# Two transformer layers with sliding-window attention on one core: all work put in order by a list scheduler, scores in 64-key blocks on row groups of the array

## The chip, the cores and the metric

The kernel runs on one core of a Trainium2 chip. The metric is device microseconds of one launch, the median of several runs. The core has five engines with queues of their own: PE (TensorE, matrix products into PSUM), ACT (ScalarE), DVE (VectorE), POOL (GpSimd) and SP (which here only issues DMAs). Each engine runs its instructions in the order in which they were written, and waits on semaphores for the others.

## The reference

Two passes over x of 2048 rows by 512 features, each of an attention block and a feed-forward block with the same weights:

```python
def _A_ref(x, wqkv, wo):          # x normed; H = 32, Dh = 16, W = 256
    q, k, v = ...                 # x @ wqkv, split in 32 heads of 16
    scores = einsum("bhqd,bhkd->bhqk", q, k) * Dh ** -0.5
    mask = (idx[:, None] - idx[None, :] >= 0) & (idx[:, None] - idx[None, :] < W)
    p = softmax(where(mask, scores, -1e9))
    o = einsum("bhqk,bhkd->bhqd", p, v)
    return o.reshape(B, S, D) @ wo
def _B_ref(x, w1, w2):            # Dff = 1792
    return relu(x @ w1) @ w2
x = A_x
for _ in range(2):
    x = x + _A_ref(layernorm(x), A_wqkv, A_wo)
    x = x + _B_ref(layernorm(x), B_w1, B_w2)
```

## The kernel before

x lies in SBUF as `x_sb`, 16 blocks of 128 rows by 512, fp32. The work is done in eight steps k, a chunk of 512 rows of one layer each (`NCH` = 4 chunks, two layers). A step has three parts.

- `qkv_chunk` (from L167) norms the chunk (`layer_norm_chunk`, L138), turns it with DMA transposes (L164; the first chunk on the array, L159) into `xnT`, and makes `QT`, `KT` and `Vaug` by 48 matmuls of 128x512 (L176, L184, L191), which DVE takes out of PSUM (L178, L186, L193).
- `attention_qblock` (from L205) works on 128 queries. A tile of `KT` holds 8 heads of 16 features on its 128 partitions. So that one matmul gives one head, `isolate_q` (L197) copies each head's rows of Q into `Qi`, which is zero elsewhere, by 16 DMAs a step. For each t (8 heads) and each of up to three blocks of 128 keys, two matmuls (L223) give 128 keys x (8 heads x 128 queries) in PSUM, two such buffers, and one ACT exponential of 128x1024 (L225) brings them to `pt`. POOL cuts the diagonal block and the oldest one with affine_select (L228, L232). Then 24 small matmuls a t (L240, 17 columns, with `pt` as weights) add up the product with V and the sum of the exponentials. DVE divides (L247, L248), three DVE operations and two of POOL guard the result (L252 to L259).
- `attn_post` (L328) turns O by a DMA transpose (L330), multiplies it with wo (L333) and adds (L334). `ffn_chunk` (L338) norms, 56 matmuls (L346) with a ReLU on DVE (L348), 56 matmuls (L353), an addition (L355), and in the second layer the output DMA (L357).

The order is Tile's, by priority classes: scores first, then the rest of attention, then the next chunk's QKV, then the FFN of the chunk before. At the start 28 matmuls keep PE busy, ACT and DVE cast x from bf16 to fp32 (L84, L369), ACT zeroes `Qi` (L372). The last lines hold an exact way of attention, taken only if a sum of exponentials leaves its bounds (`final_flag`, L279); it is not taken here.

Of the kernel before, what the change touches and what calls it, by code (L numbers as in the profile page):

```python
# [9 lines left out]
FP32 = mybir.dt.float32  # L10
# [5 lines left out]
P = 128  # L16
NOSYNC = mybir.DependencyInfo(mybir.DependencyClass.NoSync, mybir.DependencyReason.DATA)


@with_exitstack  # L20
def kernel(
# [32 lines left out]
    CLS = {"setup": 0, "s": 1, "a": 2, "q": 3, "f": 4}
    counters = {k: 0 for k in CLS}
    cur_cls = [None]

    class prio:
        def __init__(self, cls):
            self.cls = cls  # L60
        def __enter__(self):
            self.prev = cur_cls[0]
            if self.prev is not None:
                counters[self.prev] = tc.cur_priority - CLS[self.prev] * 10_000_000
            cur_cls[0] = self.cls
            tc.cur_priority = CLS[self.cls] * 10_000_000 + counters[self.cls]
        def __exit__(self, *a):
            counters[self.cls] = tc.cur_priority - CLS[self.cls] * 10_000_000
            cur_cls[0] = self.prev
            if self.prev is not None:  # L70
                tc.cur_priority = CLS[self.prev] * 10_000_000 + counters[self.prev]

    with prio("setup"):
        nc.scalar.preload_act_table_set("natural_log_exp_and_others")
        x_sb = const.tile([P, NB, D], FP32, name="x_sb")
        x_in = A_x.rearrange("b (n p) d -> p (b n) d", p=P)
        wqkv = const.tile([P, KC, 3 * D], BF16, name="wqkv")
        wqkv_in = A_wqkv.rearrange("(kc p) n -> p kc n", p=P)
        xst0 = work.tile([P, 4, D], BF16, name="xst0", tag="xnT", bufs=1)
        nc.sync.dma_start(xst0[:], x_in[:, 0:4, :])  # L80
        for part in range(3):
            nc.sync.dma_start(wqkv[:, :, part * D:(part + 1) * D], wqkv_in[:, :, part * D:(part + 1) * D])
        for j in range(4):
            nc.scalar.copy(x_sb[:, j, :], xst0[:, j, :])  # L84
        Qi = [const.tile([P, 4, 8, 256], BF16, name=f"Qi{i}") for i in range(2)]
        wo = const.tile([P, KC, D], BF16, name="wo")
        nc.scalar.dma_start(wo[:], A_wo.rearrange("(kc p) n -> p kc n", p=P))
        w1 = const.tile([P, KC, DFF], BF16, name="w1")
        nc.scalar.dma_start(w1[:], B_w1.rearrange("(kc p) n -> p kc n", p=P))
        w2 = const.tile([P, NF, D], BF16, name="w2")  # L90
        nc.scalar.dma_start(w2[:], B_w2.rearrange("(f p) n -> p f n", p=P))
        nc.gpsimd.tensor_scalar(out=wqkv[:, :, 0:D], in0=wqkv[:, :, 0:D], scalar1=0.25, scalar2=1.0,
                                op0=ALU.mult, op1=ALU.mult)

        LN_PRESCALE = 2.0 ** -40
# [12 lines left out]

    ident = const.tile([P, P], BF16, name="ident")
    with prio("setup"):  # L110
        make_identity(nc, ident[:])
    with prio("f"):
        warm = ps_w.tile([P, 512], FP32, name="warm", tag="ps_w")
        for _ in range(N_WARMUP):
            nc.tensor.matmul(warm[:], lhsT=ident[:], rhs=ident[:].rearrange("p (o q) -> p o q", o=1).to_broadcast([P, 4, P]),
                             start=True, stop=True)
    ones_bf = const.tile([P, P], BF16, name="ones_bf")
    hm = const.tile([P, 8], FP32, name="hm")
    maskbias = const.tile([P, 3, P], FP32, name="maskbias")

    def fallback_constants():
        nc.vector.memset(ones_bf[:], 1.0)
# [5 lines left out]
        nc.vector.memset(maskbias[:], 0.0)  # L128
# [5 lines left out]

    last_startup_act = [None]

    def layer_norm_chunk(c, xnT, sfx, startup=False, j0=0, j1=4):
        mv4 = small.tile([P, 4, 2], FP32, name="mv4" + sfx)  # L138
        for j in range(j0, j1):
            b = 4 * c + j  # L140
            st = small.tile([P, 6], FP32, name="st" + sfx)
            nc.vector.bn_stats(out=st[:], in_=x_sb[:, b, :])
            nc.vector.bn_aggr(out=mv4[:, j, :], in_=st[:])  # L143
        lnv = small.tile([P, 4], FP32, name="lnv" + sfx)
        rstd = small.tile([P, 4], FP32, name="rstd" + sfx)
        with prio("setup"):
            nc.scalar.activation(lnv[:, j0:j1], mv4[:, j0:j1, 1], ACT.Ln, bias=ln_bias[:], scale=LN_PRESCALE)  # L147
            nc.scalar.activation(rstd[:, j0:j1], lnv[:, j0:j1], ACT.Exp, bias=exp_bias[:], scale=-0.5)
        nb = small.tile([P, 4], FP32, name="nb" + sfx)
        nc.vector.scalar_tensor_tensor(out=nb[:, j0:j1], in0=mv4[:, j0:j1, 0], scalar=-1.0, in1=rstd[:, j0:j1],  # L150
                                       op0=ALU.mult, op1=ALU.mult)
        for j in range(j0, j1):
            b = 4 * c + j
            xn = work.tile([P, D], BF16, name="xn" + sfx, bufs=2)
            if startup:
                nc.scalar.activation(xn[:], x_sb[:, b, :], ACT.Identity, bias=nb[:, j:j + 1], scale=rstd[:, j:j + 1])
                tp = ps_d.tile([P, KC, P], BF16, name="tp", tag="ps_d")
                for kc in range(KC):
                    nc.tensor.transpose(tp[:, kc, :], xn[:, kc * P:(kc + 1) * P], ident[:])  # L159
                last_startup_act[0] = nc.scalar.copy(xnT[:, :, j * P:(j + 1) * P], tp[:])  # L160
            else:
                nc.gpsimd.tensor_scalar(out=xn[:], in0=x_sb[:, b, :], scalar1=rstd[:, j:j + 1],  # L162
                                        scalar2=nb[:, j:j + 1], op0=ALU.mult, op1=ALU.add)
                nc.sync.dma_start_transpose(out=xnT[:, :, j * P:(j + 1) * P],  # L164
                                            in_=xn[:].rearrange("p (kc d) -> p kc d", kc=KC))
# [275 lines left out]
```

## Time and profile before

| | us |
|---|---|
| three runs | 641.25, 642.2 (median), 643.69 |
| span of the profiled execution | 643.3 |
| PE, ACT, POOL, DVE busy | 576.2, 368.2, 367.7, 321.1 |
| mean granted clock of PE, of full speed | 0.970 |
| first exponential, last exponential's group, last matmul (start) | 28.7, about 568, 634.4 |

No other time is listed for the profiled execution; its span lies among the three runs. In the rows, PE is the matmul and PEld its weight load. A matmul's duration runs from issue to its modelled end, and matmuls overlap, so the pitch of a row of them is read from a row's whole length. "idle before <- X" is the time for which the engine stood still, and what ended it.

### The profile page before, as it was taken

The numbers are of one execution on the slowest core, as the hardware profiler recorded it, in microseconds if no ns is written. First come the engines' busy times: TensorE is split into PE (matmuls) and PEld (weight loads), VectorE is DVE, ScalarE is ACT, GpSimd is POOL, SyncE is SP. The second block draws the span as 40 slices with busy tenths as digits, with TensorE's granted clock in tenths as the row PEclk, the third lists the DMA queues.
The fourth block names the chain that finished last, engine by engine and source line by source line (L and its number), as shares of the span: only waits on it lengthen the run. The fifth ranks groups of instructions, "written<-read, shape, count | busy, mean of one in ns | idle before, by whom it ended". The sixth has DMA issues, their size and how long they took to land.

```text
span 643.3 us, 12352 instructions
## 1 busy us (share of the span) xinstructions
PE 576.2 (90%) x5053; PEld 282.8 (44%) x5053; DVE 321.1 (50%) x701; ACT 368.2 (57%) x407; POOL 367.7 (57%) x391
## 2 busy tenths in 40 slices
PE   6957979999989999999899999999998899979994
PEld 2323434544544444534453444534454344534442
DVE  2794533544465634476455634475443544436361
ACT  5667686999850399705870399705894079920000
POOL 2168778888861287815872287814887147851200
PEclk8968996999999999999999999999999999999998
DMA  9601121111002110102101110202102210131302
GB/s 316 202 22 34 31 55 42 26 34 43 10 9 42 45 31 10 43 8 50 34 11 41 42 34 11 42 10 52 23 10 57 36 25 9 19 59 16 58 8 39
DMA packets 69217, 27.10 MB, mean 42 GB/s; under 512 B 52512, under 2 KB 68640, under 8 KB 69152
## 3 DMA queue, kind: packets, MB, share of 16 engines
q1 hardware_dynamic: 63984, 19.94, 13.6%
q0 software_dynamic: 2304, 2.10, 2.2%
q10 hardware_dynamic: 2864, 4.19, 1.8%
q8 instruction: 41, 0.67, 0.5%
q14 instruction: 24, 0.20, 0.1%
HBM read 7.86 MB, written 2.10 MB: 15 GB/s over the span
## 4 chain that ended last, share of the span: by engine, by line
PE 32%; POOL 19%; DMA 11%; issue 10%; ACT 8%; DVE 4%; SPq 0%; POOLq 0%; ACTq 0%
DMA OT<-O 9%; ACT pt L225 8%; PE ps_d L353 7%; POOL pt L228 7%; PE Sps L223 5%; PE ps_d L346 5%; POOL O L259 4%; POOL pt L232 4%; PE ps_w L333 3%; PE ps_d L176 3%; PE acc L240 3%; PE ps_d L184 3%; PE ps_d L191 3%; POOL O L257 2%; DMA xn2T<-xnB 1%
## 5 line engine op out<-in xcount | busy, mean ns | idle before, releaser
L225 ACT ACTIVATE pt<-Sps 128x1024 bf16<-128x1024 f32 x360 | 344.8, 1025 | 95.3 <-PE Sps L223 82.8
L223 PE MATMUL Sps<-Qi,KT 128*128 128x512 bf16 x720 | 218.9, 386 | 4.1 <-ACT pt L225 2.8
L228 POOL TENSOR_SCALAR_AFFINE_SELECT pt<-pt 128x1024 bf16<-128x1024 bf16 x128 | 140.3, 1099 | 67.4 <-ACT pt L225 67.1
L232 POOL TENSOR_SCALAR_AFFINE_SELECT pt<-pt 128x1024 bf16<-128x1024 bf16 x112 | 122.2, 1091 | 34.4 <-ACT pt L225 31.4
L240 PEld LDWEIGHTS <-pt 128*128 128x128 bf16 x2880 | 100.2, 96 | 87.6 <-POOL pt L228 38.4
L240 PE MATMUL acc<-Vaug,pt 128*128 128x17 bf16 x2880 | 108.9, 171 | 26.4 <-POOL pt L228 20.7
L346 PE MATMUL ps_d<-xn2T,w 128*128 128x512 bf16 x448 | 123.9, 378 | 0.9 <-DVE hT L348 0.9
L348 DVE TENSOR_SCALAR hT<-ps_d 128x512 bf16<-128x512 f32 x112 | 77.1, 689 | 61.4 <-PE ps_d L346 61.0
L353 PE MATMUL ps_d<-w,hT 128*128 128x512 bf16 x448 | 105.7, 381 | 0.0
L223 PEld LDWEIGHTS <-KT 128*128 128x128 bf16 x720 | 64.3, 97 | 68.5 <-issue 16.8
L334 DVE TENSOR_TENSOR x_sb<-ps_w,x_sb 128x512 f32<-128x512 f32 x32 | 22.1, 692 | 102.2 <-PE ps_w L333 80.8
L353 PEld LDWEIGHTS <-hT 128*128 128x128 bf16 x448 | 43.2, 98 | 50.4 <-issue 1.9
L346 PEld LDWEIGHTS <-w 128*128 128x128 bf16 x448 | 39.8, 97 | 43.2 <-issue 5.7
L333 PE MATMUL ps_w<-wo,OT 128*128 128x512 bf16 x128 | 38.3, 390 | 18.4 <-DMA OT<-O 18.3
L162 POOL TENSOR_SCALAR xnB<-x_sb,rstdB,nbB 128x512 bf16<-128x512 f32 x32 | 24.4, 766 | 42.4 <-DMA xn2T<-xnB 25.5
L247 DVE RECIPROCAL chk<-acc 128x16 f32<-128x16 f32 x64 | 16.4, 256 | 56.8 <-PE acc L240 56.7
L162 POOL TENSOR_SCALAR xnA<-x_sb,rstdA,nbA 128x512 bf16<-128x512 f32 x28 | 21.4, 769 | 40.2 <-DVE nbA L150 37.7
L178 DVE CAST QT<-ps_d 128x512 bf16<-128x512 f32 x32 | 22.0, 689 | 37.2 <-PE ps_d L176 37.2
L147 ACT ACTIVATE lnvB<-mv4B,ln_bias 128x4 f32<-128x4 f32 x8 | 2.4, 296 | 66.2 <-DVE mv4B L143 66.2
L357 POOL DMA_DIRECT2D out_dram<-x_sb x16 | 9.1, 570 | 52.8 <-DVE x_sb L355 37.2
L176 PE MATMUL ps_d<-xnT,wqkv 128*128 128x512 bf16 x128 | 36.4, 399 | 2.6 <-DVE QT L178 1.8
L355 DVE TENSOR_TENSOR x_sb<-ps_d,x_sb 128x512 f32<-128x512 f32 x32 | 22.0, 689 | 28.4 <-PE ps_d L353 25.8
(62 smaller groups left out, 391.5 us busy)
## 6 DMA issues: line engine op xcount, KB each, us to landing
Qi<-QT SPq DMA_DIRECT2D x128, 32.0 KB, 2.0
w<-in_B_w_dram ACTq DMA_DIRECT2D x2, 1792.0 KB, 13.9
xst<-in_A_x_dram SPq DMA_DIRECT2D x4, 512.0 KB, 14.4
out_dram<-x_sb POOLq DMA_DIRECT2D x16, 128.0 KB, 2.3
wqkv<-in_A_wqkv_dram SPq DMA_DIRECT2D x3, 512.0 KB, 13.1
wo<-in_A_wo_dram ACTq DMA_DIRECT2D x1, 512.0 KB, 5.5
OT<-O SPq DMA_TRANSPOSE x32, 2.3
xn2T<-xnB SPq DMA_TRANSPOSE x32, 2.4
```

Of the source, the lines that this page charges most:

```text
L162: nc.gpsimd.tensor_scalar(out=xn[:], in0=x_sb[:, b, :], scalar1=rstd[:, j:j + 1], scalar2=nb[:, j:j + 1], op0=ALU.mult, op1=ALU.add)
L176: nc.tensor.matmul(ps[:], lhsT=wqkv[:, kc, t * P:(t + 1) * P], rhs=xnT[:, kc, :], start=(kc == 0), stop=(kc == KC - 1))
L223: nc.tensor.matmul(Sps[:, xh].rearrange("p j q -> p (j q)"), lhsT=KT[:, t, kcols], rhs=Qih[:, t, 4 * xh:4 * xh + 4, qcols], start=True, st ...
L225: nc.scalar.activation(pt[:, kbi].rearrange("p j q -> p (j q)"), Sps[:].rearrange("p x j q -> p (x j q)"), ACT.Exp)
L228: nc.gpsimd.affine_select(out=pt[:, 2], in_=pt[:, 2], pattern=[[0, 8], [1, P]], compare_op=ALU.is_ge, fill=0.0, base=0, channel_multiplier=-1)
L232: nc.gpsimd.affine_select(out=pt[:, 0], in_=pt[:, 0], pattern=[[0, 8], [-1, P]], compare_op=ALU.is_gt, fill=0.0, base=0, channel_multiplier=1)
L240: mm = nc.tensor.matmul(acc[:, h % 16, :], lhsT=pt[:, kbi, j, :], rhs=Vaug[:, slot(layer, kb), h, :], start=(ii == 0), stop=(ii == len(kbi ...
L259: nc.gpsimd.tensor_tensor(out=O3, in0=O3, in1=ok[:].to_broadcast([P, 32, 16]), op=ALU.mult)
L333: nc.tensor.matmul(ps[:], lhsT=OT[:, kc, :], rhs=wo[:, kc, :], start=(kc == 0), stop=(kc == KC - 1))
L346: nc.tensor.matmul(ps[:, n0:n1], lhsT=w1[:, kc, f * P:(f + 1) * P], rhs=xnT[:, kc, n0:n1], start=(kc == 0), stop=(kc == KC - 1))
L348: nc.vector.tensor_relu(hT[:, f, n0:n1], ps[:, n0:n1])
L353: nc.tensor.matmul(ps[:], lhsT=hT[:, f, j * P:(j + 1) * P], rhs=w2[:, f, :], start=(f == 0), stop=(f == NF - 1))
```

## The change

The whole body is written anew; what is computed stays.

- Scores. K is kept as `KBD`: for 64 keys and one group of 32 partitions (two heads), the 64 columns of the even head and the 64 of the odd one, each zero on the other head's rows (`spread_k` does this out of PSUM with a mask of the partition's parity; two operations). A score matmul has 32 rows, 128 columns (2 heads x 64 keys) and streams up to 512 queries; four of them, one a group of 32 partitions, write four PSUM banks. Q is used as it is. A unit is one t and 512 queries (256 in the first and the last step, `HALVED`); its 12 blocks of 64 keys are packed in five groups (`FULL`; three in `HALF`) of at most 512 columns, in which only the queries lie that see the keys. There is one score buffer of four banks, so a group's scores wait for the exponential of the group before.
- One exponential takes a group, up to 128x2048. The triangles are cut by a minimum with a table on DVE or by affine_select on POOL.
- P times V: for two heads at once, 128 (2 heads x 64 keys) x 128 queries as weights, 34 columns, up to six key blocks; 2880 matmuls as before.
- O is turned on PE (`transpose`) and copied by DVE or ACT; the norm's 1/sqrt is a power on POOL; no Ln and Exp on ACT. The guards of O are gone, the check at the end stays.
- The input's bf16 lies in the upper half of each fp32 row of `x_sb` (`x_raw`) until the first addition; the casts are gone.
- `Qi`, its zeroing and its DMAs are gone.
- Every operation is an `Op` with the engines that may run it and a time on each, with constants for links between engines. A loop over these times chooses per engine the operation of least key, and writes the instructions in that order, which a chain of dependencies then fixes on each engine. Four PSUM banks are shared by all but the scores. Where PE would stand for 0.4 us by these times, a matmul without use is put in.

```diff
-        nc.sync.dma_start(xst0[:], x_in[:, 0:4, :])
-        for j in range(4):
-            nc.scalar.copy(x_sb[:, j, :], xst0[:, j, :])
-            cv = nc.vector.tensor_copy(x_sb[:, b, :], xst[:, b - 4, :])
-            mz = nc.scalar.memzero(Qi[i][:])
-            nc.sync.dma_start(out=Qi[hfq][16 * j:16 * j + 16, :, j, :],
-        nc.sync.dma_start_transpose(out=OT[:], in_=O[:].rearrange("p (kc d) -> p kc d", kc=KC))
...
+FULL = [
+    [(-1, 0, 4, 0), (4, 4, 4, 4)],
+    [(1, 1, 5, 0), (-2, 0, 3, 5)],
+    [(5, 5, 3, 0), (0, 0, 5, 3)],
+    [(3, 3, 5, 0), (-3, 0, 2, 5), (-4, 0, 1, 7)],
+    [(7, 7, 1, 0), (6, 6, 2, 1), (2, 2, 5, 3)],
+]
...
+    def x_raw(b0, b1):
+        return x_sb[:, b0:b1, D // 2:D].bitcast(BF16)
...
+    for h in range(2):
+        sp.dma_start(x_raw(2 * h, 2 * h + 2), x_in[:, 2 * h:2 * h + 2, :])
+    for part in (1, 0, 2):
+        sp.dma_start(wqkv[:, :, part * D:(part + 1) * D], wqkv_in[:, :, part * D:(part + 1) * D])
...
+    def spread_k(e, layer, c, t, h0, h1, ps):
...
+            for p in range(2):
+                o = KBD[:, t, sa:sa + b - a, p, :]
+                i = ps[:, 64 * a:64 * b].rearrange("p (s k) -> p s k", k=64)
...
+                    dve.tensor_scalar(out=o, in0=i, scalar1=par[:, p:p + 1], scalar2=None, op0=ALU.mult)
...
+        for kb, lo, n, at in u.groups[g]:
+            sl = slot(layer, 8 * u.c + u.q0 + kb)
+            for r in range(4):
+                rows = slice(32 * r, 32 * r + 32)
+                mm(Sps[:, r, 64 * at:64 * (at + n)], KBD[rows, u.t, sl].rearrange("p e k -> p (e k)"),
+                   Qt[rows, 64 * (u.q0 + lo):64 * (u.q0 + lo + n)], True, True)
...
+        act.activation(places(pb, g)[:, :, 64 + a:64 + z], Sps[:, :, a:z], ACT.Exp, scale=0.25)
...
+        dve.tensor_tensor(out=v, in0=v, in1=w, op=ALU.min)
...
+        for p in range(4):
+            for i, kb in enumerate(kbs):
+                g, lo, at = u.place[kb]
+                col = (4 * g + p) * PW + 64 + 64 * (at + 2 * jl - lo)
+                mm(acc[:, p], Pb[pb][:, col:col + P], V2[:, slot(u.k // NCH, 8 * u.c + u.q0 + kb), :, 4 * u.t + p, :],
+                   i == 0, i == len(kbs) - 1)
...
+        return op(key, {"POOL": (0.72, lambda: pool.tensor_tensor(out=r, in0=r, in1=mhalf[:, j0:j1], op=ALU.pow))}, deps)
...
+            box.ps = box.tile([P, KC, P], BF16, "tp")
+            for kc in range(KC):
+                pe.transpose(box.ps[:, kc, :], src()[:, kc * P:(kc + 1) * P], ident[:])
...
+                    cell["S"] = ps_s.tile([P, 4, 512], FP32, name="Sps")
+                    score_group(u, g, Q[u.k, u.t], pb, cell["S"])
+                scores[s] = op(-1e5 + s, {"PE": (0.22 + 0.02 * len(u.groups[g]) + cols * 0.00042, sfn)},
+                               need + ([exps[s - 1]] if s else []))
...
+                if t - idle_since[0] >= (0.4 if t > 20 else 0.0) and sum(1 for f, _ in psum.free if f <= t) > 1:
...
+                    d.opts = {"PE": (d.opts["PE"][0], lambda box=box: mm(
+                        box.tile([P, 512], FP32, "warm")[:], ident[:],
```

## Rows read from the trace of the kernel before

**Rows 1.** The page, part 1: busy us (share of the span) and instructions by engine

```profile
PE 576.2 (90%) x5053; PEld 282.8 (44%) x5053; DVE 321.1 (50%) x701; ACT 368.2 (57%) x407; POOL 367.7 (57%) x391
```

**Rows 2.** Busy time by stretch: length, PE, PEld, DVE, ACT, POOL, granted clock, DMA

```profile
28.00:60.00 32.00, 20.43 (x196) 9.11 (x195) 23.41 (x59) 21.45 (x27) 22.30 (x23) 0.79 0.15 34
...
160.00:526.00 366.00, 341.00 (x3020) 168.72 (x3018) 191.02 (x412) 207.54 (x231) 213.99 (x223) 1.00 0.14 30
...
579.00:634.00 55.00, 55.00 (x246) 23.91 (x245) 27.24 (x41) 0.59 (x2) 7.86 (x13) 0.98 0.19 30
```

**Rows 3.** Groups of PE instructions, 160 to 526 us: busy, mean ns | idle before, releaser

```profile
L223 PE MATMUL Sps<-Qi,KT 128*128 128x512 bf16 x426 | 126.3, 378 | 0.9
...
L240 PE MATMUL acc<-Vaug,pt 128*128 128x17 bf16 x1705 | 64.0, 171 | 9.9 <-POOL pt L228 9.9
L333 PE MATMUL ps_w<-wo,OT 128*128 128x512 bf16 x76 | 22.0, 382 | 11.5 <-DMA OT<-O 11.5
L176 PE MATMUL ps_d<-xnT,wqkv 128*128 128x512 bf16 x80 | 20.5, 377 | 1.8 <-DVE QT L178 1.8
```

**Rows 4.** Timeline, 236 to 256 us: start, length, engine, line, count, idle before

```profile
246.29 0.87 PEld L240 LDWEIGHTS <-pt 128*128 128x128 bf16 x24
246.50 0.76 PE L240 MATMUL acc<-Vaug,pt 128*128 128x17 bf16 x24
...
247.11 0.59 PE L223 MATMUL Sps<-Qi,KT 128*128 128x512 bf16 x2
...
248.66 0.38 PE L346 MATMUL ps_d<-xn2T,w 128*128 128x512 bf16 x1
...
254.69 0.59 PE L223 MATMUL Sps<-Qi,KT 128*128 128x512 bf16 x2
255.33 1.02 ACT L225 ACTIVATE pt<-Sps 128x1024 bf16<-128x1024 f32 x1 [0.26 <-PE Sps L223]
```

**Rows 5.** Timeline, 575 to 643 us: the last FFN and the end

```profile
622.32 12.25 PE L353 MATMUL ps_d<-w,hT 128*128 128x512 bf16 x56
...
634.40 0.17 PE L283 MATMUL cnt_ps<-chk_bb,ones_bf 128*128 128x1 bf16 x1
```

**Rows 6.** Timeline, 0 to 30 us: the start

```profile
5.87 1.14 ACT L84 CAST x_sb<-xst 128x512 f32<-128x512 bf16 x2 [3.78 <-DMA xst<-in_A_x_dram]
...
6.52 1.29 DVE L142 BATCH_NORM_STATS2 stA<-x_sb 128x6 f32<-128x512 f32 x2 [3.28 <-ACT x_sb L84]
...
11.84 0.59 ACT L160 COPY xnT<-tp 128x512 bf16<-128x512 bf16 x1
11.96 0.34 PEld L159 LDWEIGHTS <-xnA 128*128 128x128 bf16 x4 [0.43 <-ACT xnA L156]
11.96 0.61 PE L159 MATMUL tp<-ident,xnA 128*128 128x128 bf16 x4 [0.17 <-ACT xnA L156]
...
15.95 4.79 PE L176 MATMUL ps_d<-xnT,wqkv 128*128 128x512 bf16 x16 [0.67 <-ACT xnT L160]
```

**Rows 7.** Timeline, 28 to 40 us: first exponentials, the casts, a stop of PE

```profile
28.66 6.52 ACT L225 ACTIVATE pt<-Sps 128x1024 bf16<-128x1024 f32 x7 [5.74 <-PE Sps L223]
28.96 8.56 DVE L369 CAST x_sb<-xst 128x512 f32<-128x512 bf16 x12
29.73 0.59 PE L223 MATMUL Sps<-Qi,KT 128*128 128x512 bf16 x2 [0.90 <-ACT pt L225]
...
39.39 0.58 PE L240 MATMUL acc<-Vaug,pt 128*128 128x17 bf16 x16 [5.40 <-DVE O L248]
```

**Rows 8.** Groups of instructions of the whole span, by line and shape

```profile
L225 ACT ACTIVATE pt<-Sps 128x1024 bf16<-128x1024 f32 x360 | 344.8, 1025 | 95.3 <-PE Sps L223 82.8 <-POOL pt L232 6.2 <-POOL xnA L162 3.0
...
L228 POOL TENSOR_SCALAR_AFFINE_SELECT pt<-pt 128x1024 bf16<-128x1024 bf16 x128 | 140.3, 1099 | 67.4 <-ACT pt L225 67.1
...
L348 DVE TENSOR_SCALAR hT<-ps_d 128x512 bf16<-128x512 f32 x112 | 77.1, 689 | 61.4 <-PE ps_d L346 61.0
...
L248 DVE TENSOR_TENSOR O<-acc,chk 128x256 bf16<-128x256 f32 x64 | 26.6, 416 | 1.9 <-DVE chk L247 0.4
...
L247 DVE RECIPROCAL chk<-acc 128x16 f32<-128x16 f32 x64 | 16.4, 256 | 56.8 <-PE acc L240 56.7
...
L372 ACT ACTIVATE Qi<-Qi 128x4096 uint32<-128x4096 uint32 x2 | 7.1, 3612 | 0.0
```

**Rows 9.** Two lines' own view (L252, L254): ns of one, least/median/most

```profile
L252 DVE TENSOR_TENSOR ok<-chk,c_hi x32: 180/422/1007, 41.1 to 572.1; 128x32 f32<-128x32 f32 x32
...
L254 DVE TENSOR_TENSOR ok<-chk,c_lo x32: 177/180/1080, 41.2 to 572.2; 128x32 f32<-128x32 f32 x32
```

More of the change, by code (lines that the diff above doesn't have):

```diff
@@ L54 @@
[L54 to L71, printed above, removed]
@@ L109 @@
[L109 to L117, printed above, removed]
-    hm = const.tile([P, 8], FP32, name="hm")
@@ new lines, with op, landed @@
+    ops = []
+    def op(key, opts, deps=(), take=None, uses=(), keep=0):
+        uses = list(uses) + ([take] if take is not None and take not in uses else [])
+        return Op(key, opts, deps, take, uses, keep)
+    psum = Pool("p", 4, ps_d)
+    xns = Pool("xn", 3, work)
+    stg = Pool("stg", 3, work)
+    ots = Pool("OT", 3, work)
+    def landed(t):
+        o = Op(0, {}, [], None, [], 0)
+        fixed.append((o, t))
+        return o
+    fixed = []
+    d_x = [landed(5.0), landed(5.4)]
@@ new lines, with copy @@
+    d_w = {1: landed(7.4), 0: landed(9.0), 2: landed(10.6)}
+    d_xc = {c: landed(10.6 + 1.7 * c) for c in range(1, NCH)}
+    d_wo, d_w1, d_w2 = landed(18.0), landed(24.0), landed(30.0)
+    def copy(e, o, i, relu=False):
+        if e == "ACT":
+            act.activation(o, i, ACT.Relu if relu else ACT.Copy)
+        elif e == "POOL":
+            pool.tensor_copy(o, i)
+        elif relu:
+            dve.tensor_relu(o, i)
+        else:
+            dve.tensor_copy(o, i)
+    EVAC = {512: {"DVE": 0.66, "ACT": 0.59}, 256: {"DVE": 0.42, "ACT": 0.38}}
@@ new lines, with push, offer @@
+    import heapq
+    ENGINES = ("PE", "ACT", "DVE", "POOL", "SP")
+    busy = {e: (1.9 if e == "PE" else 1.5) for e in ENGINES}
+    ready = {e: [] for e in ENGINES}
+    events, done_ops, seq = [], [0], [0]
+    def push(t, o, e):
+        seq[0] += 1
+        heapq.heappush(events, (t, seq[0], o, e))
+    def offer(o):
+        for e in o.opts:
+            ready[e].append((o.at(e), o))
+            push(o.at(e), None, None)
+    for o, t in fixed:
+        push(t, o, "SP")
+    for o in ops:
+        if o.left == 0 and o.opts:
+            offer(o)
@@ new lines, with choose @@
+    started, last_act, idle_since, log = set(), [None], [1.9], []
+    score_next = [0]
+    def choose(e, t):
+        best = None
+        for at, o in ready[e]:
+            if at > t + 1e-9 or (o.take is not None and sum(1 for f, _ in o.take.pool.free if f <= t + 1e-9) <= o.keep):
+                continue
+            if e == "ACT" and o.key > -9e4 and not act_free(t):
+                continue
+            key = (o.key, o.number) if e == "PE" else (at + o.key, o.number)
+            if best is None or key < best[0]:
+                best = (key, o)
+        return None if best is None else best[1]
@@ new lines, in act_free, with begin @@
+    def act_free(t):
+        s = score_next[0]
+        if last_act[0] == "exp" or s >= len(line):
+            return True
+        return scores[s].number not in started and (scores[s].left > 0 or scores[s].at("PE") > t)
+    def begin(e, t, o):
+        started.add(o.number)
+        for x in o.opts:
+            ready[x] = [r for r in ready[x] if r[1] is not o]
+        if o.take is not None:
+            free = sorted(o.take.pool.free)
+            o.take.index = free[0][1]
+            o.take.pool.free = free[1:]
+        us, fn, *total = o.opts[e]
+        fn()
+        busy[e] = t + us
+        if e == "ACT":
+            last_act[0] = "exp" if o.key < -9e4 else "copy"
+            if o.key < -9e4:
+                score_next[0] += 1
+        log.append((t, e, us, o))
+        push(t + (total[0] if total else us), o, e)
+        push(t + us, None, None)
@@ L133, in fallback_constants @@
                                 fill=NEG, base=0, channel_multiplier=1)
[L135 to L165, printed above, removed]
```

877 lines of the change are left out of this document (609 added, 268 removed).

## The prediction

> **What bounds it now.** First the page's busy times [rows 1]: PE has 90% of the span, ACT and POOL 57% each, DVE 50%. An average can hide stages, so next the busy time by stretch [rows 2]. In the middle, 160 to 526 us, which is five of the eight steps, PE works 341.0 of 366 us at the full clock, ACT 207.5. At the end, 579 to 634 us, PE works without a stop on the last FFN, and ACT does nothing. Only from 28 to 60 us does PE stand for a third of the time. Then who ends PE's idle time [rows 3]: of 25 us in the five steps, 11.5 us go to the DMA that turns O, 9.9 to POOL's masks, and only 0.9 fall to the scores, which wait for a buffer that ACT frees. PE bounds the kernel, by its own work. So the question of the change is how much PE time it takes away, and whether the new order feeds PE as well.
>
> The pitches of PE, from the timeline: 56 matmuls of 512 columns in 12.25 us, the last one 0.38 long [rows 4, 5], so (12.25 - 0.38) / 55 = 0.216 us each. Of P times V, 24 in 0.76 us, the last of 0.17 [rows 3, 4]: (0.76 - 0.17) / 23 = 0.026; their weight loads are at (0.87 - 0.10) / 23 = 0.033. Sum before: 1408 dense matmuls (384 QKV, 128 wo, 896 FFN) x 0.216 = 304; 720 scores x 0.216 = 156; 2880 x 0.026 to 0.033 = 75 to 95; together 535 to 555, with 8 of warm-up. The page's 576 agrees, since a busy time counts each drain.
>
> **The scores.** A full unit has 40 squares of 64 keys by 64 queries for each pair of heads (the third entries of the table), 30 in a layer's first chunk; 4 x (40 x 3 + 30) x 2 = 1200 for all, packed in 164 groups (24 whole units of five, 20 in the first step, 24 in the last). A full group is eight squares, 512 columns, so there is the work of 150 full groups. No row shows matmuls on row groups of 32. Bounds: if the four run beside each other at no extra cost, a group takes one matmul's pitch, 0.216, in sum 32 us. If they run one after the other, 4 x 0.216 = 0.864, 130 us, and if PE also drains where the shape changes, on both sides of a group, twice 0.17 more (what a matmul lasts beyond its pitch [rows 4]), 164 x 0.34 = 56, 186 us. I take them as beside each other, with one drain exposed: the 0.38 of a lone matmul plus three more starts of 0.026, 0.46 a group, 75 us over 164; this is nearest to the row of a lone matmul, and half full groups cost less. Removed are 156, gained 81.
> The rows cannot show the drain by itself. The Trainium skill (TensorEngine Tiling (Array Packing), Key Properties) says that a change of tiling mode drains TensorE, which speaks against a kernel that changes shape 328 times; by it the sum would be up to the 56 above higher than with no drain, and no run here shows it yet.
>
> **P times V** keeps its 2880 matmuls. 34 columns in place of 17 are 0.014 us at the dense pitch per column, still under the 0.026 pitch that 17 columns had [rows 4], so columns cost nothing. I take 0.027 (bursts of 24 on one PSUM tile), 78 us; bounds 74 and 95.
>
> **O turned on the array.** 40 sets of four transposes on PE (32 of O, 4 each for the first and the last chunk's norm; only the first 4 are there now). One set took 0.61 at the start at the low clock, four loads 0.34 [rows 6]; I take 0.35 x 40 = 14 us, bounds 8 and 24. The removed DMA gives back its 11.5 us of PE idle in five steps; the copy out of PSUM is on DVE or ACT, where there is room (below).
>
> PE's work after: 304 + 78 + 75 + 14 = 471 us.
>
> **PE's idle time.** Start: the first QKV matmul now comes at 15.95 us, the first exponential at 28.66 [rows 6, 7]. After: x in two halves, landed at about 5.5 (cast at 5.87 now), no cast, statistics of two blocks 1.6, the power on POOL 0.5 (no row shows one; 0.2 to 1.1, a small and a large POOL operation), two norms 0.9, transposes and copy 1.2: the first K matmul at about 10; K, its spreading and scores 2.2, so the first exponential at about 12.5. Between, PE has only a half chunk to work on, I add 4. Idle 14. The casts, with the PE stop of 5.4 at 39 us [rows 7], are gone, as is the zeroing on ACT.
> End: from PE's last matmul to the end of the span are now 8.9 us [rows 5], kept as 9. Before the last half FFN (12 us of PE) the last mask, division, copies, addition, statistics, power and norm stand in a chain in which PE has nothing else: 6. Idle 15.
> In the loop: 25 of 366 us now; without the wait on O's DMA 13.5, that is 3.7%; of 455 us in the loop 17. The sum is made of PE's stretches in one execution, whose span (643.3) is 0.2% above the median.
>
> Sum: 471 + 14 + 15 + 17 = 517, say **515 us**.
>
> **Is there a new bound?** ACT first, as there is one score buffer and a chain exponential, scores, exponential. A column costs (3612 - 1025) / 3072 = 0.84 ns [rows 8], so 2048 take 1.89 us; in all 1200 x 256 x 0.84 ns = 259 and 164 x 0.16 fixed = 285 us. Between, scores and ACT follow each other's end within 0.05 us [rows 4, 7]; with 0.46 for the scores and 0.15 for the matmul that PE is in, the chain is 285 + 164 x 0.1 + 75 + 25 = 401, and with start and end 443: under 515. In its gaps of some 0.7 us ACT can make a copy of 0.59 [rows 6], 20 a step. DVE: 0.69 a PSUM tile of 512 [rows 8]. A step has 14 ReLUs, 4 Q, 8 for K, 4 V, 4 of O, 8 additions (42, 29 us), 16 divisions (0.26 and 0.42 now, half the columns after, so 0.5), 8 statistics at 0.85 (0.65 [rows 6] and a second small operation), some 34 masks, estimated at 0.5 from the 0.42 of 256 elements: 61 us, of which ACT can take 12; POOL takes masks, V's spreading and norms. In a step of some 60 us no one engine is full, but DVE is not far from it.
>
> **Rivals.**
> 1. *PE's cost is at its lower bounds* (scores 0.30, small matmuls 0.026, order with 1% idle): 304 + 75 + 49 + 10 + 29 + 5 = 472. For it: list order has dense matmuls ready at nearly all times, ACT's chain allows it.
> 2. *The row groups do not overlap, or PE drains at each change.* Scores at 0.86 are 55 to 66 us more, with drains 111 more: 570 to 626. The chain of ACT would be 443 + 66 to 111, so still under PE. Still faster than before, hardly at the end.
> 3. *The fixed order does not fit the chip.* Times in the planner that are off let an engine's first instruction wait while the next could run. Idle of 13% in the loop in place of 3.7%: 42 us more, 557. For it: before, the masks held PE for 9.9 us in five steps, and the shared PSUM has four banks.
> 4. *Slower than before: masks behind POOL.* A mask on DVE reads two SBUF operands. Such operations of 32 elements last 0.18 us alone and up to 1.08 [rows 9], the length of a POOL mask beside them (1.10 [rows 8]). P times V waits for its masks at the head of PE's queue, and behind it are the next scores and so the next exponential. If each of the 164 groups stood for 1.1 us, that is 180 us, less the 17 of idle already counted: 678. It decides from (642 - 515 + 17) / 164 = 0.88 us a group. Against it: the medians are 0.42 and 0.18, and the POOL masks that PE had to wait for cost 9.9 us in five steps, with more POOL work than now (guards of O and masks of 1024 columns leave).
> The Trainium skill (SBUF — State Buffer, the summary's row on DVE beside GpSimd) says that a VectorE operation with two SBUF inputs and a GpSimd one that reads SBUF block each other wholly; the greatest times of the row agree, the medians show that they seldom meet.
>
> That the change does not do what it says would show as rival 2, or as the exact way being taken, which nothing suggests.
>
> **Chances.** Forecast, 490 to 545: 0.52. Rival 1: 0.18. Rival 3: 0.14. Rival 2: 0.11. Rival 4: 0.05. About 0.5% is what a measurement of this kernel can tell from no change, so faster 0.93, same 0.02, slower 0.05. The range takes in most of rivals 1 and 3 and the nearer half of 2: 475 to 585.
>
> **What would show it.** A group of scores from first start to last end near 0.46 (rival 2: over 0.9). P times V at 24 in under 0.8. PE busy above 90% from 20 us to the last FFN, at the full clock; ACT idle between exponentials, waiting for PE's scores. If instead PE waits mostly for the exponentials, ACT's chain is the bound and the time is nearer 450 to 480. PE waits on DVE or POOL masks of over 40 us in sum would be rival 3 or 4. The first exponential near 12.5 us; the last half FFN in the final 25 us. It is wrong if PE's clock falls in the loop: from 28 to 60 us, with PE two thirds busy, the granted clock was 0.79 [rows 2], so gaps that last would cost dense matmuls too.

## The result, and the profile after

The changed kernel takes 517.67 us (median of 4 runs, 516.55 to 518.3) against 642.78: a ratio of 0.806, with a 95% interval of 0.804 to 0.808. The forecast was 515, in 475 to 585. The profiled execution took 517.21 us, with a span of 515.2 us at a mean granted clock of 0.989.

The page, part 1 (busy us, share of the span, instructions), answering to [rows 1]:

```profile
PE 480.3 (93%) x6202; PEld 258.2 (50%) x6202; DVE 363.5 (71%) x990; ACT 363.1 (70%) x332; POOL 302.5 (59%) x673
```

PE lost 96 us of work and has a larger share of a shorter span. Where it still stands shows by stretch, answering to [rows 2] (columns: length, PE, PEld, DVE, ACT, POOL, granted clock, DMA share, GB/s):

```profile
0.00:20.00 20.00, 15.11 (x114) 8.11 (x115) 14.82 (x47) 10.70 (x20) 12.23 (x27) 1.00 0.93 316
20.00:60.00 40.00, 28.48 (x426) 16.91 (x425) 33.00 (x101) 24.14 (x25) 26.58 (x61) 0.87 0.23 60
60.00:240.00 180.00, 171.00 (x2336) 92.11 (x2334) 132.09 (x358) 137.76 (x112) 114.03 (x254) 1.00 0.09 18
240.00:420.00 180.00, 177.20 (x2318) 91.18 (x2315) 139.30 (x371) 137.11 (x113) 113.96 (x256) 1.00 0.11 22
420.00:480.00 60.00, 60.00 (x821) 31.67 (x820) 34.56 (x92) 41.06 (x36) 34.38 (x76) 1.00 0.10 26
...
480.00:515.20 35.20, 28.47 (x198) 18.22 (x196) 9.78 (x25) 12.32 (x30) 1.33 (x2) 0.98 0.07 21
```

From 60 to 480 us PE works 408.2 of 420 us at the full clock, and no other engine exceeds 78% in any of the three stretches. The hole is at 20 to 60 us, where PE has 28.5 of 40.

Not all of PE's busy time is useful. The new planner puts in dummy matmuls where no work is ready (tile `warm`):

```profile
L106 PE MATMUL warm<-ident 128*128 128x512 bf16 x73 | 21.1, 411 | 2.1 <-POOL ident masks.py:199 1.5 <-DVE O L106 0.6
```

Of these 21.1 us, 7.7 lie before 20 us, 2.2 from 20 to 60, 11.2 from 60 to 420. So PE's useful work is 480.3 - 21.1 = 459 us, and it lacks work for 515.2 - 459 = 56 us.

The timeline of a stretch in the loop, answering to [rows 4] (start, length, engine, line, count, idle before):

```profile
241.13 0.81 PE L106 MATMUL ps_d<-xnT,wqkv 128*128 128x512 bf16 x3
...
241.88 0.40 PE L106 MATMUL Sps<-Qt,KBD 32*128 32x320 bf16 x12
...
242.21 1.25 PE L106 MATMUL ps_d<-xnT,wqkv 128*128 128x512 bf16 x5
...
242.38 1.88 ACT L106 ACTIVATE Pb<-Sps 128x2048 bf16<-128x2048 f32 x1 [0.94 <-PE Sps L106]
...
248.56 0.39 PE L106 MATMUL tp<-ident,O 128*128 128x128 bf16 x4
...
249.31 0.32 PE L106 MATMUL Sps<-Qt,KBD 32*128 32x320 bf16 x4
...
249.56 1.99 PE L106 MATMUL acc<-V2f,Pb 128*128 128x34 bf16 x72
```

Twelve score matmuls hold PE from 241.88 to 242.21, 0.33 us, which is also the median of the 164 groups, from a group's first start to the next matmul; they sum to 53.8. A group also starts late: from the first of the three dense matmuls to the scores are 0.75 us, of which two pitches are 0.43 and the third lasts 0.32, not 0.216. Over the groups this entry costs about 0.095, so a group takes 0.43, and all 164 take 53.8 + 15.6 = 69 us. The four row groups do work beside each other. The exponential idled 0.94 us, waiting for the scores: ACT waits for PE.

All that PE waited for in the span (total us, times, longest), the largest first:

```profile
PE acc L106 <- DVE V2f L106: 5.6, 2, 5.0
PE Sps L106 <- ACT Pb L106: 3.1, 7, 1.2
PE ps_d L106 <- DMA xnT<-xn: 2.8, 3, 1.0
PE ps_d L106 <- DMA xn2T<-xn: 2.5, 2, 1.5
PE acc L106 <- POOL Pb L106: 2.4, 3, 1.5
```

Waits on the exponentials (3.1) and on POOL's masks (2.4; 9.9 in five steps before [rows 3]) are small. The largest is one stop of 5.0 us, and the timelines of PE and DVE show its place:

```profile
27.46 0.19 PE L106 MATMUL acc<-V2f,Pb 128*128 128x34 bf16 x1 [5.02 <-DVE V2f L106]
```
```profile
21.51 0.66 DVE L106 BATCH_NORM_STATS2 st<-x_sb 128x6 f32<-128x512 bf16 x1
...
23.12 0.11 DVE L106 MEMSET V2f<- 64x64 bf16 x1 [0.26 <-issue]
...
26.41 1.79 DVE L106 COPY V2f<-Vst 64x256 bf16<-64x256 bf16 x4
```

The ones in V's padded tile come on DVE behind the norm statistics of later chunks, which nobody needs yet, and the copies of V come behind the ones.

### The profile page after: what moved, and what is told of

Same layout as the page of the kernel before. It is cut to its first block, busy times and chain, and to the rows that moved or that the text cites. A ratio compares the mean times of both kernels' runs of the same rounds, so it can differ in the third digit from the quotient of the medians.

```text
span 515.2 us, 14925 instructions
## 1 busy us (share of the span) xinstructions
PE 480.3 (93%) x6202; PEld 258.2 (50%) x6202; DVE 363.5 (71%) x990; ACT 363.1 (70%) x332; POOL 302.5 (59%) x673
## 4 chain that ended last, share of the span: by engine, by line
PE 61%; POOL 5%; DVE 2%; DMA 2%; issue 1%; ACT 1%; POOLq 0%
PE ps_d L106 44%; PE acc L106 10%; PE Sps L106 6%; POOL Pb L106 3%; DMA xn2T<-xn 2%; PE tp L106 1%; POOL xn L106 1%; ACT Pb L106 1%; POOL rstds L106 1%; POOL nbs L106 1%; DVE xn L106 0%; DVE V2f L106 0%; DVE st L106 0%; DVE KBD L106 0%; DVE x_sb L106 0%
## 5 line engine op out<-in xcount | busy, mean ns | idle before, releaser
L106 ACT ACTIVATE Pb<-Sps 128x2048 bf16<-128x2048 f32 (+4 forms) x164 | 284.1, 1732 | 97.5 <-PE Sps L106 63.5
L106 POOL TENSOR_SCALAR_AFFINE_SELECT Pb<-Pb 64x256 bf16<-64x256 bf16 x530 | 233.0, 440 | 155.1 <-ACT Pb L106 133.2
L106 PE MATMUL ps_d<-xn2T,w 128*128 128x512 bf16 (+1 forms) x560 | 111.5, 337 | 3.6 <-DMA xn2T<-xn 2.5
L106 PE MATMUL ps_d<-w,hT 128*128 128x512 bf16 x448 | 109.1, 380 | 0.0
L106 PE MATMUL acc<-V2f,Pb 128*128 128x34 bf16 x2880 | 87.6, 178 | 12.9 <-DVE V2f L106 5.6
L106 PEld LDWEIGHTS <-Pb 128*128 128x128 bf16 x2880 | 82.9, 96 | 32.9 <-POOL Pb L106 9.9
L106 DVE TENSOR_TENSOR Pb<-Pb,tri 128x512 bf16<-128x512 bf16 (+1 forms) x131 | 54.3, 416 | 27.0 <-ACT Pb L106 25.9
L106 PEld LDWEIGHTS <-w 128*128 128x128 bf16 x560 | 50.6, 97 | 42.0 <-issue 7.9
L106 PE MATMUL ps_d<-xnT,wqkv 128*128 128x512 bf16 (+1 forms) x288 | 67.6, 356 | 3.2 <-DMA xnT<-xn 2.8
L106 PE MATMUL Sps<-Qt,KBD 32*128 32x192 bf16 (+4 forms) x1536 | 62.5, 249 | 4.9 <-ACT Pb L106 3.1
L106 DVE TENSOR_SCALAR hT<-ps_d 128x512 bf16<-128x512 f32 (+1 forms) x82 | 49.3, 605 | 21.0 <-PE ps_d L106 20.3
L106 PEld LDWEIGHTS <-hT 128*128 128x128 bf16 x448 | 40.0, 98 | 44.7 <-issue 3.6
L106 PEld LDWEIGHTS <-KBD 32*128 32x128 bf16 x1536 | 25.6, 92 | 57.6 <-issue 54.8
L106 DVE BATCH_NORM_STATS2 st<-x_sb 128x6 f32<-128x512 f32 (+1 forms) x64 | 43.7, 683 | 4.0 <-DMA x_sb<-in_A_x_dram 3.5
L106 ACT ACTIVATE hT<-ps_d 128x256 bf16<-128x256 f32 (+1 forms) x58 | 28.2, 486 | 21.9 <-PE ps_d L106 20.5
L106 DVE RECIPROCAL chk<-acc 128x8 f32<-128x8 f32 x128 | 25.8, 202 | 22.9 <-PE acc L106 21.3
L106 DVE TENSOR_TENSOR x_sb<-ps_d,x_sb 128x512 f32<-128x512 f32 x48 | 32.5, 685 | 12.3 <-PE ps_d L106 11.6
L106 DVE TENSOR_TENSOR O<-acc,chk 128x128 bf16<-128x128 f32 x128 | 37.3, 291 | 4.4
L106 DVE COPY V2f<-Vst 64x256 bf16<-64x256 bf16 x108 | 37.9, 351 | 2.6 <-ACT Vst L106 1.0
L106 PEld LDWEIGHTS <-wqkv 128*128 128x128 bf16 x288 | 24.8, 97 | 28.0 <-issue 6.9
L106 POOL TENSOR_TENSOR rstds<-rstds,mhalf 128x2 f32<-128x2 f32 (+1 forms) x33 | 23.4, 712 | 19.1 <-DVE rstds L106 17.6
L106 PE MATMUL ps_d<-wqkv,xnT 128*128 128x512 bf16 x128 | 33.6, 386 | 0.0
```

Source lines behind the costliest of these rows:

```text
L106: inst = fn(*a, **k)
```

## The experiments

All were timed in three rounds beside the kernel before, whose median was 643.0 to 644.7 us. Unless it says otherwise, an edit is made to the changed kernel. The diffs are cut to the lines that tell what an edit does, and long lines break off.

### Whose work is the time? The scores before, and the row groups after

The kernel before, with one of its two score matmuls, the exponential reading that one twice:

```diff
-                        for xh in range(2):
+                        for xh in range(1):
                             nc.tensor.matmul(Sps[:, xh]
```

> The kernel before with one of the two score matmuls of each block left out (the exponential reads the other half twice, so four of eight heads have another head's scores). 360 x 0.216 = 78 us of PE work go, all else stays: nearly the PE time that the new scores save. Theory (PE's own work bounded it, and most of the gain is the scores' PE time): 565 to 585 us. Rival (the gain is the planned order's, and before waits on masks, DMA and ACT would come forward): 600 to 640 us.

Measured: 562.5 us, 82 less, for 360 x 0.216 = 78 us less PE work. The kernel before was bound by PE one for one; its masks and O's DMA did not turn up as the next bound.

The changed kernel with all four score matmuls of a square on the first 32 partitions:

```diff
-                rows = slice(32 * r, 32 * r + 32)
+                rows = slice(0, 32)
```

> The changed kernel with all four score matmuls of a block on the first 32 partitions of K and Q (the four banks get the same scores, so six of eight heads have another head's). Instructions, columns, banks and order stay; only the row groups are the same. If the gain comes from row groups beside each other, a full group now lasts 4 x 0.213 = 0.85 us and more in place of 0.33 (a loop exchange that left two of a row group in a row cost nothing, so it is not the order). Theory (PE's time, as summed): 0.52 to 0.6 more for 150 full groups, of which a part falls in waits of PE: 560 to 605 us. Rival (PE gives back most of it in other waits, as it did when 24 us of it were taken away and only 7 came out): 530 to 550 us.

Measured: 598.0 us, 80 more. Its timeline of PE:

```profile
293.94 0.36 PE L106 MATMUL acc<-V2f,Pb 128*128 128x34 bf16 x8
294.23 1.05 PE L106 MATMUL Sps<-Qt,KBD 32*128 32x64 bf16 x12
295.21 1.04 PE L106 MATMUL ps_d<-wo,OT 128*128 128x512 bf16 x4
```

A group lasts 0.98 us in place of 0.33 (both medians of 164; sums 154.6 and 53.8). So working side by side is worth 101 us of PE time and 80 us of the whole. This is what rival 2 would have looked like: 598 is in its 570 to 626. Here the scores hold PE no shorter than before the change (154.6, against 156 by pitch), and the kernel still gains 45 us: that much is left for the order and all else that changed.

The four row groups one after the other, in place of key block by key block:

```diff
-        for kb, lo, n, at in u.groups[g]:
-            sl = slot(layer, 8 * u.c + u.q0 + kb)
-            for r in range(4):
+        for r in range(4):
+            for kb, lo, n, at in u.groups[g]:
+                sl = slot(layer, 8 * u.c + u.q0 + kb)
```

> The changed kernel with the two loops of a score group exchanged, row group outside and key block inside: the same matmuls, but mostly two of the same row group follow each other. Theory (row groups run beside each other, and PE bounds the kernel): a full group grows from some 0.33 to 0.6 to 0.75 us from its first start to the next matmul, 150 groups, so 555 to 580 us. Rival (the four never overlapped, or the scores are hidden behind ACT): 515 to 525 us.

Measured: 520.1 us, a ratio of 0.808 (0.805 to 0.812), hardly apart from the change. The expected loss is not there:

```profile
243.36 0.81 PE L106 MATMUL ps_d<-xnT,wqkv 128*128 128x512 bf16 x3
244.10 0.42 PE L106 MATMUL Sps<-Qt,KBD 32*128 32x320 bf16 x12
244.46 1.25 PE L106 MATMUL ps_d<-xnT,wqkv 128*128 128x512 bf16 x5
```

The group takes 0.36 here, 0.34 in the median of 164. With three matmuls of one row group written ahead of those of the next, they overlap all the same: what counts is on which rows the work lies, not in which order it is written. The single starts in this trace show how. In the group above, the first matmuls of the four row groups (320 columns each) start 10 ns apart, as the first four do in the median of all groups of twelve. The two others of each row group, though written ahead of the next row group's first, start 147 ns in and later.

### PE's work, more and less

A fifth w1 matmul added to each four, and one of four left out, both in the changed kernel's order; then one of four left out with the planner told of it (only there is the order new):

```diff
+                    for again in range(2 if kc == 1 else 1):
                         mm(ps[:, n0:n1], w1[:, kc, f * P:(f + 1) * P], ...)
```
```diff
+                    if kc < KC - 1:
                         mm(ps[:, n0:n1], w1[:, kc, f * P:(f + 1) * P], ...)
```
```diff
-                box, m = group(d0 + (d1 - d0) * f / (2 * NF), KC, 0.000422
+                box, m = group(d0 + (d1 - d0) * f / (2 * NF), KC - 1, 0.000422
```

> The changed kernel with a fifth matmul in every tile of x w1 (one quarter of the sum is counted twice), not told to the planner: 24 us more of PE work, order as before. Theory (PE's work bounds it and what is added counts in full): 539 to 545 us. Rival (PE's waits on the other engines take up half, as when 24 us were taken away): 524 to 532 us.

> The changed kernel without the last of the four matmuls of every tile of x w1 (84 of 512 and 56 of 256 columns left out, so h lacks a quarter of its sum); the planned order of the rest stays. By pitch 84 x 0.216 + 56 x 0.109 = 24 us less PE work. Theory (PE bounds it): 492 to 499 us. Rival (ACT's chain or the evacuations bound it): 512 to 518 us.

> The kernel without the last matmul of every tile of x w1, this time with the planner told, so that it makes an order for 24 us less PE work. With the order unchanged the 24 us had given 7.4. Theory A (the fixed order kept PE from using the time, since the other engines' work lies where it was planned for the longer PE): 492 to 500 us. Theory B (ACT's chain, DVE or the exchange between layers is the next bound whatever the order): 505 to 511 us.

Measured: 539.95 us, 22.3 more for 24 us of PE work; 510.2, only 7.4 less for 24; and 515.0 (511.8 to 517.3), 2.7 less. Added work counts in full. Taken away, it gives a third, and with a new order almost nothing, which neither theory expected.

For the old order the two profiles add up: the span falls by 6.3, PE's busy time by 14.9 and not by 24, and its idle time grows by 8.6. Most of the missing 9 us of busy time can be the clock's. Stretches of 10 us of the kernel with three (columns as above):

```profile
60.00:70.00 10.00, 10.00 (x141) 6.81 (x140) 7.59 (x25) 7.41 (x7) 3.14 (x7) 0.83 0.01 2
90.00:100.00 10.00, 8.01 (x131) 5.60 (x131) 5.90 (x18) 5.90 (x7) 3.60 (x9) 0.83 0.30 56
130.00:140.00 10.00, 7.27 (x135) 4.59 (x133) 3.62 (x13) 5.29 (x3) 4.84 (x11) 0.83 0.33 43
270.00:280.00 10.00, 8.19 (x98) 3.95 (x97) 6.44 (x19) 5.31 (x6) 4.28 (x11) 0.83 0.35 68
```

At 0.83 about a third of the stretch is at the lower level, 1.2 GHz. Over the span the mean clock is 0.975, against 0.989: (1 - 0.975) x 508.9 - (1 - 0.989) x 515.2 = 7 us more that a full clock would have saved at most. Three of the four stretches have PE busy for 7.3 to 8.2 us and DMA at 0.30 to 0.35: PE waits at the step changes for the norm's way round by DMA, 6.0 us in all where it was 2.8. That is 3.2 of the 8.6 us of new idle time; waits for DVE's O are another 3.1 (5.1 in place of 2.0). The first three waits:

```profile
PE acc L106 <- DVE V2f L106: 6.7, 2, 6.1
PE ps_d L106 <- DMA xnT<-xn: 6.0, 5, 2.0
PE Sps L106 <- ACT Pb L106: 3.8, 11, 1.2
```

Elsewhere, beside the first half of the FFN, there are places where ACT has no gap to speak of in its timeline:

```profile
284.67 1.88 ACT L106 ACTIVATE Pb<-Sps 128x2048 bf16<-128x2048 f32 x1 [0.21 <-PE Sps L106]
...
286.44 0.59 ACT L106 ACTIVATE hT<-ps_d 128x512 bf16<-128x512 f32 x1
...
286.60 0.29 PE L106 MATMUL Sps<-Qt,KBD 32*128 32x256 bf16 x4 [0.23 <-ACT Pb L106]
```

An exponential and a ReLU fill the turn, and here it is PE that waits for ACT. Over the span this is little: 3.8 us where it was 3.1, so ACT is not the limit that took the rest. With the new order the clock is lower still, 0.971, and the lows lie in and behind the gaps:

```profile
120.00:130.00 10.00, 7.13 (x77) 2.96 (x77) 4.08 (x11) 5.06 (x3) 6.86 (x16) 0.91 0.43 56
130.00:140.00 10.00, 9.49 (x133) 5.66 (x135) 6.56 (x20) 6.35 (x5) 3.61 (x9) 0.75 0.01 2
...
150.00:160.00 10.00, 6.53 (x59) 2.75 (x59) 6.71 (x17) 4.58 (x6) 6.61 (x16) 0.66 0.27 29
```

PE is busy for 7.1 of 10 us, and in the next 10 us, with 9.5 of 10 busy, half of the time is at 1.2 GHz. What PE waits for most in the new order is POOL's masks, 8.0 us where the old order with three had 3.2:

```profile
PE acc L106 <- POOL Pb L106: 8.0, 6, 1.9
```

Why the planner's new order has more gaps than the old one with holes in it was not settled. It plans against one time for each matmul, and a matmul at the lower clock takes longer (0.38 and 0.43 us from start to start at 135 us of the first kernel with three, in place of 0.216); that this is the cause is not shown.

### Is ACT's chain the bound?

The exponential of a group in four instructions; and the exponentials and masks of two of four row groups only:

```diff
-        act.activation(places(pb, g)[:, :, 64 + a:64 + z], Sps[:, :, a:z], ACT.Exp, scale=0.25)
+        for r in range(4):
+            act.activation(places(pb, g)[:, r, 64 + a:64 + z], Sps[:, r, a:z], ACT.Exp, scale=0.25)
```
```diff
-        act.activation(places(pb, g)[:, :, 64 + a:64 + z], Sps[:, :, a:z], ACT.Exp, scale=0.25)
+        act.activation(places(pb, g)[:, 0:2, 64 + a:64 + z], Sps[:, 0:2, a:z], ACT.Exp, scale=0.25)
```

> The changed kernel with each exponential split in four, one for each row group; the order of all else and PE's work stay. ACT's chain per full group grows by 0.2 to 0.5 us (four fixed parts of 0.16 in place of one, partly overlapped), over 164 groups 30 to 80 us. Theory (PE's own work bounds it, ACT's chain ends some 70 us earlier): 517 to 530 us. Rival (the one score buffer's chain exponential, scores, exponential bounds it): 550 to 600 us.

> The changed kernel with exponentials and masks of two of the four row groups only; the product with V reads these two twice, so heads of the other two get another head's weights. PE's instructions stay as they are; ACT loses some 130 us, DVE and POOL half of their mask work. Theory (PE bounds it): 505 to 516 us, what is left of PE's waits. Rival (ACT's chain, or masks that hold PE): 390 to 450 us.

Measured: 518.1 us with ACT 29 us busier (392.3), no change. With half the exponentials 509.15: ACT falls by 125 us to 238.3, POOL by 77 to 225.9, the time by 8.5. The stretch of 60 to 240 us, first of the four instructions, then of the half:

```profile
60.00:240.00 180.00, 170.63 (x2321) 92.05 (x2319) 131.53 (x353) 147.35 (x294) 112.17 (x251) 0.99 0.09 18
```
```profile
60.00:240.00 180.00, 174.95 (x2382) 93.84 (x2381) 122.91 (x362) 89.83 (x113) 85.94 (x262) 0.99 0.10 18
```

ACT goes from 137.8 up to 147.4 and down to 89.8, and PE stays at 171 to 175. The chain has slack. What 8.5 us there are may as well be the masks' as the exponentials': this run halves both.

### The parts: order, O, masks, start

Without the order of the engines' instructions that the planner fixes (the chain that ties each instruction to the one before it):

```diff
-    chained = [True]
+    chained = [False]
```

> The changed kernel without the chain of dependencies that fixes the planner's order on each engine; the instructions are written in the planner's order, and the framework's own scheduler may move them. Theory (the order in which they are written is what counts, with PE full in most orders): 510 to 540 us. Rival (the fixed order is a large part of the gain): over 560 us.

Measured: 548.3 us, 31 more; POOL's masks are PE's first wait again, `PE acc L106 <- POOL Pb L106` with 11.2 us in 12 times. Within the change, the fixed order is worth 31 us.

O turned by DMA, as before, with the planner told its time:

```diff
-            t = transpose(-20000 + k, lambda j=j: O_of[k][:, j, :], to, ready, [ob], ob)
+            def turn(j=j, to=to):
+                sp.dma_start_transpose(out=to(), in_=O_of[k][:, j, :].rearrange(...))
+            t = op(0, {"SP": (1.22, turn, 2.6)}, ready, ob, [ob])
```

> The changed kernel with O turned by a DMA transpose again, as before the change, and the planner told of it (its own time for a DMA transpose); so 32 sets of four transposes leave PE (32 x 0.22 = 7 us) and 32 copies of 0.4 to 0.6 us leave DVE and ACT, and a DMA of 2.5 us comes into the chain of O. Theory (in a planned order other matmuls cover the DMA, so this part of the change is worth little): 510 to 520 us, the 7 us of PE given back against a longer tail. Rival (the wait on O's DMA comes back as it was, 11.5 us in five steps): 525 to 535 us.

Measured: 520.65 us (517.3 to 522.8), ratio 0.805 (0.799 to 0.811): no difference that can be told. PE waits 10.8 us in 9 times for O's DMA, and saves the transposes. That the array turns O is worth nothing measurable here.

All masks on DVE; then also V's ones early and the statistics of later chunks late (in the second diff `key`, which was 0, is 12 times the chunk's number in the first layer):

```diff
-                    times = {"DVE": 0.3 + 0.2 * (len(m) - 1), "POOL": 0.84 * len(m)}
+                    times = {"DVE": 0.3 + 0.2 * (len(m) - 1)}
```
```diff
-    c_v = [op(12, {"DVE": (0.6, lambda s0=s0: v_ones(s0))}, [c_v0[s0 // 4]]) for s0 in range(0, NSLOT, 4)]
+    c_v = [op(1, {"DVE": (0.6, lambda s0=s0: v_ones(s0))}, [c_v0[s0 // 4]]) for s0 in range(0, NSLOT, 4)]
...
-        return op(0, {"DVE": (0.85 + (0.16
+        return op(key, {"DVE": (0.85 + (0.16
```

> The changed kernel with all triangle masks on DVE; POOL, which did 530 half masks of 0.44 us, has only norms, powers and part of V left, and the planner plans anew. DVE gets some 60 us more. Theory (PE bounds it and waits for masks cost little): 512 to 524 us. Rival (masks beside each other on DVE and POOL hold PE): 500 us or less. If DVE is then the bound: 530 to 560 us.

> The kernel with all masks on DVE (7 us faster than the changed kernel), and at the start the ones of V written early and the statistics of the later chunks after the first ones' work. PE stood 5 us at 23 to 27 us for the ones of V. Theory (that wait goes and nothing takes its place): 503 to 508 us. Rival (the statistics come late for the second chunk, or ACT's chain is next): 509 to 514 us.

Measured: 510.3 us (509.5 to 511.3) and **503.1** (502.5 to 503.65), with ratios of 0.791 (0.786 to 0.795) and 0.782 (0.780 to 0.784): the second is the fastest of all, 14.6 us faster than the change. With the masks moved, POOL falls from 302.5 to 116.7 us and DVE rises only to 376.6. The planner made a new order for it, and no run separates what of the 7 us is POOL's and what the order's. The second kernel fills the hole at the start, where PE had 28.48, and 31.77 with the masks alone:

```profile
20.00:60.00 40.00, 35.41 (x544) 22.01 (x548) 36.48 (x116) 33.83 (x38) 15.21 (x33) 0.96 0.24 65
```

PE's wait for V's ones is gone from its list. Its 21st exponential starts at 62.4 us, against 69.1 with the masks alone: the 7 us are gained here and kept to the end. Which of the two edits at the start gave them was not tried apart.

## Why the prediction was right, point by point

- **The bound.** Right. PE's work was the time before (82 us for 78), and it is after (22.3 for 24; 29 us more on ACT cost nothing). What the prediction did not see is that this holds in one direction only: within some 7 us of PE time other limits come up, as the kernel with three w1 matmuls showed. So rival 1, which took off 33 us more of PE work and 12 of idle time, would have needed more than cheaper PE work.
- **Scores**, 0.46 a group and 75 us: 0.43 and 69. The rows of before could not price the drain, and it is there on both sides. On entry it is about 0.095 us. On leaving it is about 0.10: a group of one block holds PE for 0.195, 0.220 and 0.247 us at 192, 256 and 320 columns (medians; the row at 249.31 is one), where the columns at the dense pitch make 0.08, 0.11 and 0.135 and the three more starts, 3 ns apart in the trace, 0.01. Together that is some 0.2 a group and 32 us over 164, where the upper bound counted 56. The term of the sum, one drain of 0.17 exposed and three starts of 0.026, was right in size and wrong in its parts: the drain comes twice, at 0.1 each, and the starts cost next to nothing. The Trainium skill (TensorEngine Tiling (Array Packing), Key Properties) says that a change of mode drains TensorE; the trace agrees, with a late start on either side of a group.
- **P times V**, 0.027: 72 in 1.99 us, so (1.99 - 0.17) / 71 = 0.0256, 74 us in place of 78. Doubling the columns cost nothing, as forecast. **Transposes**, 0.35 a set: a set is followed by the next work after 0.22 us (248.56 to 248.78), 9 us in place of 14. The rows at hand were from the start, where the granted clock was 0.67 (9 to 16 us).
- **PE's work.** With these pitches the sum is 304 + 74 + 69 + 9 = 456, and PE's busy time without dummies is 459, in place of 471: 12 too much.
- **PE's idle time**, with dummies counted as idle, was 46 by the sum and is 56. Up to 60 us it is 26 in place of 14: the first QKV matmul came at 11.2, not 10, the first exponential at 14.65, not 12.5, and the 5.0 us stop for V's ones was in no term. The failed step is "I add 4" between them: it looked for PE's work and not at what stands in DVE's queue. The late first matmul has the same look: the first half of x had landed by 3.68 us, not 5.5, and its power on POOL was done at 6.70, but on DVE the norm's last operation starts only at 9.05, behind a zeroing of `Pb` that starts at 7.78 and takes 1.35. From 60 to 480 us it is 11.8 of idle and 11.2 of dummies, 23 of 420 us in place of 17. At the end it is 6.7 in place of 15:

```profile
496.87 6.28 PE L106 MATMUL ps_d<-xn2T,w 128*128 128x256 bf16 x56
...
502.98 6.21 PE L106 MATMUL ps_d<-w,hT 128*128 128x512 bf16 x28
509.22 0.69 DVE L106 TENSOR_TENSOR ob<-ps_d,x_sb 128x512 bf16<-128x512 f32 x1 [2.33 <-PE ps_d L106]
```

  The last half FFN is the final 12.3 us of PE, where 12 was said; but the first half stood ready to fill the chain ahead of it, and the end takes 6 us, where 8.9 [rows 5] was carried over.
- The two errors, -12 and +10, cancel. That 515 is so close is luck; its terms deserve less.
- **Rival 3** (the order does not fit) did not come: PE lacks work for 5.5% of the loop, not 13%, and waits on DVE's and POOL's masks stay under 3 us. **Rival 4** neither: PE waited 2.4 us for POOL. Its mechanism, though, is in the trace. Without a POOL instruction beside it, no mask on DVE lasts over 0.43 us. In the changed kernel 45 of 131 masks last longer than their like, by 5.9 us in all, and each of the 45 started while POOL was at work, 41 of them beside a POOL mask. With all masks on DVE it is 18 of 280 and 3.7 us, beside POOL's norms and copies of V. The extra length follows what POOL still had to do: with 0.18, 0.34 and 0.39 us left of a POOL mask, a DVE mask took 0.03, 0.19 and 0.25 us longer. So the block is real and, as PE seldom waits for a mask, too small to matter here. The prediction read from the medians of [rows 9] that the two seldom meet; for L252 that is wrong: 31 of its 32 operations had a POOL instruction beside them, and the one without took 0.18 us, where the median is 0.42. The masks on DVE in the changed kernel, and with all of them there (least/median/most ns):

```profile
L106 DVE TENSOR_TENSOR Pb<-Pb,tri x131: 277/418/873, 26.2 to 477.4; 128x512 bf16<-128x512 bf16 x84, 128x256 bf16<-128x256 bf16 x47
```
```profile
L106 DVE TENSOR_TENSOR Pb<-Pb,tri x280: 276/416/819, 22.3 to 469.4; 128x512 bf16<-128x512 bf16 x100, 128x256 bf16<-128x256 bf16 x40
```

## What to carry to other kernels

Where one engine bounds, sum its work by pitch from timeline rows, and price each new form by the pitch of the nearest row, not by the mean duration of an instruction, which counts drains that overlap. Add what a change of form costs on entry and on leaving, once a trace shows it. List the idle time by its places, and for the start read the queue of each helper engine for work that stands ahead of what the bound engine needs first; here that was worth 7 us. A planner's order has to be read as well: one had PE wait 2.4 us for POOL's masks, another 8.0. Once the engines come near to each other, work taken from the bound one pays only in part, since new gaps cost twice: as idle time, and as matmuls at the lower clock behind them.

## What the runs showed of the hardware

- Four matmuls of 32 rows on different row groups overlap in whichever order they are written: a group takes 0.33 us written in turn, 0.34 written row group by row group, 0.98 on one row group (medians of 164).
- Going from 128-row to 32-row matmuls costs some 0.1 us at the entry, and going back as much again.
- A mask on DVE that reads two SBUF operands can last longer when a POOL instruction runs at its start: 128x512 took up to 0.87 us in the changed kernel, and at most 0.43 with no POOL instruction beside it.
- The granted clock fell in and behind stretches with gaps of PE, to as low as 0.66 over 10 us, and stayed low while PE was nearly or fully busy again (0.75 with 9.49 of 10, 0.83 with 10.00). Not every gap did this: with 7.59 of 10, from 150 to 160 us of the kernel with three w1 matmuls, it was 1.00.
